# Normalizing q by an accumulating DMA and one exp, in place of transposes

## The chip, the cores and the metric

The kernel runs on one core of a Trainium2 chip. The metric is device time in microseconds of one launch. The core has engines with their own instruction queues: TensorE (PE in the profile, its weight loads PEld), VectorE (DVE), ScalarE (ACT), GpSimd (POOL), and SyncE (SP), which here only issues DMAs.

## The reference

Eight batches of a linear attention are followed by a gated projection. All is float32 on the inputs (batch 8, heads 8, tokens 576, head dimension 64); the three weights arrive as float64.

```python
q_s = q - np.max(q, axis=-1, keepdims=True)
q_s = np.exp(q_s)
q_s = q_s / (np.sum(q_s, axis=-1, keepdims=True) + 1e-09)
k_s = k - np.max(k, axis=2, keepdims=True)
k_s = np.exp(k_s)
k_s = k_s / (np.sum(k_s, axis=2, keepdims=True) + 1e-09)
kv = np.einsum('bhsd,bhse->bhde', k_s, v)
x = np.einsum('bhsd,bhde->bhse', q_s, kv)      # then [batch, token, 512 channels]
...
for k in range(5):                             # causal taps over the tokens
    gate_pre += conv_w[k] * xp[:, k:k + S, :]
gate = 1.0 / (1.0 + np.exp(-gate_pre))
val = x @ w_val
return gate * val @ w_out
```

So q is normalized over the 64 channels of a head, for each token; k over the tokens, for each channel.

## The kernel before

Batches are worked on one after the other, and a batch's later stages overlap the next batch's first ones. The 512 channels are four blocks of 128 (two heads each); the 576 tokens are 512 main ones (four chunks of 128) and a tail of 64, two batches' tails sharing one tile of 128 partitions.

**k and kv.** k's maxima over the tokens come from a channel-major copy of k (steps load_km, k_peak), pass through a DRAM row and come back broadcast to all partitions (k_row, k_spread); k_sub and k_exp then work on token-major k. Batches 0 and 1 instead exponentiate the channel-major copy and transpose it on TensorE (load_kc, k_top, k_raise, k_turn). kv multiplies k by v, whose extra column of ones gives the sum; kv_norm writes kv / sum as a block-diagonal 128 x 128 tile for each channel block (tile kvd).

**q.** q is loaded token-major (load_q); q_max reduces each head, q_sub subtracts, q_exp takes exp, q_sum adds up and takes the reciprocal, q_mul scales. q_turn transposes the chunks on TensorE into PSUM (tile qTps, eight 128 x 128 transposes a group, two groups a batch), q_turned copies them to SBUF as channel-major q; tail_turn and tail_turned do the tails of two batches. Batch 0 subtracts its maximum in PSUM (q_lift, q_minus, q_raise).

**attend.** x = kvd^T q, channels on partitions and tokens along the row. For batch 0 it is one float32 product of 512 columns. For the others q and kv are split into a float32r high part and a low rest (q_turned and q_low; kv_high and kv_low) and three products are added up. The 64 tail columns are one float32 product more.

**Gate and projections.** x_high and x_low split x into float32r parts (tiles xh, xl). first and tap build the causal convolution (five taps; on DVE, or as ACT product and POOL addition), sigmoid follows. value(b, m) multiplies the four channel blocks of x by one block of w_val: 3 products x 4 blocks x 2 halves of 288 tokens = 24 matmuls (line L542). gated multiplies with the gate, g_high and g_low split again (gh, gl), project does the same 24 matmuls with w_out, store copies out of PSUM and issues the store.

**Weights.** They arrive as pairs of 32-bit words; part, field, scaled, signed and joined build float32 from them, w_high and w_low split it. Eight slabs (load_words 0 to 7), four for each matrix, and slab 8 for the taps.

**What sets the order.** ORDER, a list written out by hand, is walked from front to back; each step puts its instructions at the end of its engines' queues. A letter behind a step names its engine: a is ACT, v DVE, p POOL. All DMAs of the kernel before are issued by SP, in that order as well: one that waits for its data holds those behind it. Tile pools add waits: a step that takes a tile whose buffers are all in use waits for the last reader of the oldest. Pools that matter here are words (4 buffers; also kvs and qTlo), xh and xl (6 each), gate (6), g and o (2 each), qT (1), and PSUM's two tags "x" (attend, q_turn) and "mm" (kv, value, project), two banks each. An order step "warm n" issues n transposes that nobody reads.

## Time and profile before

| | |
|---|---|
| median of 3 runs | 321.03 us (320.58 to 323.54) |
| the profiled execution | 320.3 us, its span 318.5 us |
| granted TensorE clock, mean | 0.995 |
| busy share: PE, DVE, ACT, POOL | 93%, 85%, 64%, 59% |
| DMA moved | 51.25 MB, 161 GB/s over the span |

Busy time of an engine is the time in which it executes; a high share tells that the engine has little room, but what it is worth to relieve it depends on the stretch. The chain of waits goes back from the last instruction and puts each piece of the span down to what released it. The windows cut the span in stretches and give each engine's busy time in them, so that stretches with different limits can be told apart. In the timeline a row is one instruction, or several of one kind in a row (x2), with its start, its duration, and, in brackets, how long its engine had idled before it and what released it. Matmuls overlap in the timeline, so that their cost is read from start to start.

### The profile page before, as it was taken

How to read it: one execution, taken by the hardware profiler on the slowest of the kernel's cores; microseconds unless marked ns; L12 is line 12 of the kernel's file. 1: busy time of each engine (PE TensorE's matmuls, PEld its weight loads, DVE VectorE, ACT ScalarE, POOL GpSimd, SP SyncE). 2: the span in 40 equal slices, each digit the busy share in tenths (PEclk: the TensorE clock that was granted, in tenths of full speed). 3: DMA queues.
4: the chain of work that ended last, by engine and by line, in shares of the span. 5: the costliest groups of instructions: out<-in, count | busy, mean ns of one | idle time of the engine just before them, and what ended most of it. 6: DMA issues, size and time to landing. Idle time of an engine off the chain costs nothing.

```text
span 318.5 us, 6426 instructions
## 1 busy us (share of the span) xinstructions
PE 297.3 (93%) x2557; PEld 276.4 (87%) x2557; DVE 271.5 (85%) x374; ACT 204.6 (64%) x316; POOL 188.7 (59%) x157
## 2 busy tenths in 40 slices
PE   2897689989899989999999999999999999999995
...
GB/s 250 370 390 174 410 396 199 194 8 175 238 264 264 74 181 139 254 189 112 143 64 313 50 232 283 160 16 355 82 0 37 39 77 2 0 74 76 0 42 108
DMA packets 20525, 51.25 MB, mean 161 GB/s; under 512 B 2832, under 2 KB 7312, under 8 KB 17808
## 3 DMA queue, kind: packets, MB, share of 16 engines
...
q8 instruction: 20, 0.33, 0.4%
...
HBM read 41.39 MB, written 9.45 MB: 160 GB/s over the span
## 4 chain that ended last, share of the span: by engine, by line
PE 55%; DVE 19%; DMA 16%; issue 4%; ACT 4%; SPq 1%; DVEq 0%; ACTq 0%
PE out L542 22%; PE val L542 20%; DVE gate L524 5%; DMA km<-in_k_strided 5%; PE x L498 4%; PE kv L433 4%; DMA words<-in_w_out 3%; DMA out<-o 2%; DMA q<-in_q 2%; DMA q<-in_q_tail 2%; PE qTps L465 2%; DVE qm L347 2%; DVE g L563 2%; DVE qs L362 2%; DVE kpk L274 2%
## 5 line engine op out<-in xcount | busy, mean ns | idle before, releaser
L524 DVE SCALAR_TENSOR_TENSOR gate<-x,cw,gate 128x575 f32<-128x575 f32 (+3 forms) x99 | 78.0, 807 | 3.3 <-POOL gate L528 1.5
L528 POOL TENSOR_TENSOR gate<-gate,far 128x572 f32<-128x572 f32 (+3 forms) x29 | 39.5, 1363 | 39.2 <-ACT far L527 38.9
L542 PE MATMUL out<-gh,w_out_lo 128*128 128x288 f32 x256 | 57.0, 301 | 0.7 <-ACT gh L160 0.7
L542 PE MATMUL val<-xh,w_val_lo 128*128 128x288 f32 x256 | 56.5, 302 | 0.8 <-DVE o L162 0.7
L542 PE MATMUL out<-gl,w_out_hi 128*128 128x288 f32 x256 | 55.6, 296 | 0.9 <-DVE gl L571 0.9
L542 PE MATMUL val<-xl,w_val_hi 128*128 128x288 f32 x256 | 55.0, 296 | 0.9 <-DVE xl L518 0.9
L542 PE MATMUL out<-gh,w_out_hi 128*128 128x288 f32 x256 | 55.4, 295 | 0.0
L542 PE MATMUL val<-xh,w_val_hi 128*128 128x288 f32 x256 | 54.8, 295 | 0.0
L571 POOL TENSOR_TENSOR gl<-g,gh 128x576 fp32r<-128x576 f32 x25 | 36.8, 1476 | 29.5 <-ACT gh L160 23.1
L542 PEld LDWEIGHTS out<-gl,w_out_hi 128*128 128x128 f32 x256 | 41.4, 188 | 1.4 <-DVE gl L571 1.4
L542 PEld LDWEIGHTS val<-xh,w_val_lo 128*128 128x128 f32 x256 | 40.9, 188 | 1.8 <-DVE o L162 0.9
L542 PEld LDWEIGHTS val<-xl,w_val_hi 128*128 128x128 f32 x256 | 41.2, 188 | 1.2 <-DVE xl L518 1.2
L542 PEld LDWEIGHTS out<-gh,w_out_lo 128*128 128x128 f32 x256 | 41.2, 189 | 1.0 <-ACT gh L160 1.0
L542 PEld LDWEIGHTS out<-gh,w_out_hi 128*128 128x128 f32 x256 | 41.5, 188 | 0.0
L542 PEld LDWEIGHTS val<-xh,w_val_hi 128*128 128x128 f32 x256 | 41.3, 188 | 0.0
L389 POOL TENSOR_TENSOR q<-q,qs 128x512 f32<-128x512 f32 x25 | 26.2, 1070 | 14.7 <-DVE qs L364 14.7
L563 DVE TENSOR_TENSOR g<-val,gate 128x576 f32<-128x576 f32 x32 | 23.9, 749 | 9.9 <-PE val L542 7.3
L527 ACT ACTIVATE far<-x,cw 128x572 f32<-128x572 f32 (+3 forms) x29 | 21.0, 737 | 14.2 <-DVE gate L524 9.3
L160 ACT CAST gh<-g 128x576 fp32r<-128x576 f32 x25 | 16.7, 672 | 17.5 <-DVE g L563 17.4
L160 ACT COPY o<-out 128x576 f32<-128x576 f32 (+1 forms) x22 | 13.5, 618 | 22.1 <-PE out L542 12.1
L531 ACT ACTIVATE gate<-gate 128x576 f32<-128x576 f32 x32 | 21.6, 685 | 6.1 <-DVE gate L524 3.5
L289 POOL TENSOR_TENSOR k<-k,kmax 128x512 f32<-128x512 f32 x18 | 24.9, 1397 | 0.9 <-DMA kmax<-krow 0.9
...
## 6 DMA issues: line engine op xcount, KB each, us to landing
...
q<-in_q SPq DMA_DIRECT2D x7, 1024.0 KB, 7.4
...
k<-in_k SPq DMA_DIRECT2D x6, 1024.0 KB, 7.5
...
words<-in_w_out SPq DMA_DIRECT2D x4, 512.0 KB, 11.8
```

Source lines behind the costliest of these rows:

```text
L160: nc.scalar.copy(out=out, in_=in_)
L289: engine(e).tensor_sub(kk[r, cs], kk[r, cs], mx[r, cs])
L389: engine(e).tensor_mul(qq, qq, s.unsqueeze(2).broadcast_to([P, H, D]))
L433: nc.tensor.matmul(acc[h * D:(h + 1) * D, p, :], T["k", b][:, c, cs] if c < 4 else ktz[b % 2][:, cs], T["v", b][:, c, hd] if c < 4 else T[ ...
L498: nc.tensor.matmul(ps[:, :MAIN], a, z, start=(i == 0), stop=(i == len(parts) - 1))
L524: nc.vector.scalar_tensor_tensor(out=a, in0=x, scalar=w, in1=a, op0=ALU.mult, op1=ALU.add)
L527: nc.scalar.activation(part, x, AF.Copy, scale=w)
L528: nc.gpsimd.tensor_add(a, a, part)
L531: nc.scalar.activation(T["gate", b, p], T["gate", b, p], AF.Sigmoid)
L542: nc.tensor.matmul(ps[:, cs], a[:, kb, ms], z[kb][:, cs], start=(kb == 0 and i == 0), stop=(kb == NB - 1 and i == 2),)
L563: nc.vector.tensor_mul(T["g", b, m], T["val", b, m], T["gate", b, m])
L571: engine(e).tensor_sub(T["gl", b, m], T["g", b, m], T["gh", b, m].bitcast(F32))
```

## The change

**q, batches 2 to 7.** Token-major q is still loaded, and q_max, q_sub, q_exp and q_sum still run, but only for the numbers: q_log takes the logarithm of the sums (ACT) and combines it with the maxima to -(max) - log(sum) (DVE). q_row transposes these numbers (at most 40 columns) on TensorE, copies them to SBUF and writes them to DRAM rows by four small DMAs of SP (and two more for the tails of a pair). q_in loads raw q again, channel-major, 1.18 MB, into the tile qTs (two buffers). q_spread adds the numbers to it by two DMAs issued from POOL's queue, which read each row broadcast to the 64 channels of its head. q_last takes exp of the tile, 2304 elements a partition. Since exp(q - max - log(sum)) is the normalized value, q_mul, q_turn, q_turned, q_low and the tail steps go for these batches.

**attend, all batches.** Two float32 products of 288 columns each (kvd times the whole channel-major q), in place of the three float32r products of 512 and the tail's 64; kv_high and kv_low go.

**Batches 0 and 1.** They keep the transposes of q. Batch 0's path through PSUM goes; q_max, q_exps and q_sum work on pieces of q that are loaded in another order. Each of the two batches has its own tail_turn.

**Buffers and tables.** The f tiles (load_km, weight parts) have four buffers and not three; xh and xl are halves of one "pair" tile, whose six buffers the weight words use as well; g and o have three. Maxima that are needed negated come negated from the reduction. One set of ACT tables that holds exp and logarithm is loaded by name ahead of the first use after a sigmoid.

**The order.** ORDER is written anew throughout. Three places show it. The first is DVE around the last steps of batch 0 ahead of its first value product. Before (gate is tap of batch 0 in its channel block, xl is x_low, e are weight words, ks is kv_norm of batch 1):

```order
L249 TENSOR_SCALAR e_350<-e_350 128x512
L250 SCALAR_TENSOR_TENSOR e_350<-words_348,e_350 128x512
L524 SCALAR_TENSOR_TENSOR gate_0_417<-x_0_399,cw,gate_0_417 128x572
L524 SCALAR_TENSOR_TENSOR gate_2_512<-x_2_462,cw,gate_2_512 128x575
L249 TENSOR_SCALAR e_391<-e_391 128x512
L250 SCALAR_TENSOR_TENSOR e_391<-words_203,e_391 128x512
L518 TENSOR_TENSOR xl_2_535<-x_2_462,xh_2_522 128x576
L443 TENSOR_SCALAR ks_539<-kv_465 128x4
L444 RECIPROCAL ks_539<-ks_539 128x4
L524 SCALAR_TENSOR_TENSOR gate_2_512<-x_2_462,cw,gate_2_512 128x574
L518 TENSOR_TENSOR xl_3_555<-x_3_515,xh_3_531 128x576
```

After (qm is q_max of batch 2, kpk is k_peak of batch 2, x_0_1 <- x_1 is x_low of channel block 1):

```order
L352 TENSOR_REDUCE qm_463<-q_410 128x40
L511 SCALAR_TENSOR_TENSOR gate_1_432<-x_1_402,cw,gate_1_432 128x572
L278 TENSOR_REDUCE kpk_149<-km_2_420 128x1
L511 SCALAR_TENSOR_TENSOR gate_1_432<-x_1_402,cw,gate_1_432 128x573
L505 TENSOR_TENSOR x_0_1_438<-x_1_402,x_0_1_438 128x576
L511 SCALAR_TENSOR_TENSOR gate_1_432<-x_1_402,cw,gate_1_432 128x574
L511 SCALAR_TENSOR_TENSOR gate_1_432<-x_1_402,cw,gate_1_432 128x575
L511 SCALAR_TENSOR_TENSOR gate_0_446<-x_0_423,cw,gate_0_446 128x573
L511 SCALAR_TENSOR_TENSOR gate_0_446<-x_0_423,cw,gate_0_446 128x574
L253 TENSOR_SCALAR e_428<-e_428 128x512
L254 SCALAR_TENSOR_TENSOR e_428<-words_375,e_428 128x512
L511 SCALAR_TENSOR_TENSOR gate_0_446<-x_0_423,cw,gate_0_446 128x575
```

The whole of q_max 2 and a k_peak of batch 2 stand ahead of batch 0's taps and of x_low; x_low of blocks 0, 3 and 2 follow in rows 73, 77 and 78 of DVE's list, where before the last one is row 70.

The second place is TensorE from the end of a projection to batch 2's first attend. Before it is preceded by transposes; these are the rows from batch 1's last value product before its attend (val is value 0 3, x_0 and x_1 are attend):

```order
L542 MATMUL val_3_697<-xh_3_531,w_val_hi 128x288 x2
L542 MATMUL val_3_697<-xl_3_555,w_val_hi 128x288 x2
L498 MATMUL x_0_730<-qT_695,kvs_594 128x512 x2
L498 MATMUL x_0_730<-qTlo_0_728,kvs_594 128x512
L499 MATMUL x_0_730<-qTt_375,kvd_80 128x64
L498 MATMUL x_1_755<-qT_695,kvs_594 128x512 x2
L498 MATMUL x_1_755<-qTlo_0_728,kvs_594 128x512
L499 MATMUL x_1_755<-qTt_375,kvd_80 128x64
L542 MATMUL out_0_790<-gh_0_675,w_out_lo 128x288 x2
```

After, the end of project 0 1 and attend 2 0, with the next value product behind it:

```order
L530 MATMUL out_1_1042<-gl_2_758,w_out_hi 128x288 x2
L530 MATMUL out_1_1042<-gh_3_811,w_out_lo 128x288 x2
L530 MATMUL out_1_1042<-gh_3_811,w_out_hi 128x288 x2
L530 MATMUL out_1_1042<-gl_3_837,w_out_hi 128x288 x2
L486 MATMUL x_0_1072<-qT_699,kvd_78 128x288 x2
L530 MATMUL val_0_1081<-x_1_0_829,w_val_lo 128x288 x2
L530 MATMUL val_0_1081<-x_1_0_829,w_val_hi 128x288 x4
```

An attend has two matmuls, not four, reads kvd and one tile of q, and no transposes of q stand among the batches from 2 on.

The third place is POOL around the first accumulating DMA. Before, the end of batch 0's g_low (gl), with kv_low (kvs) and q_sub of batch 2 (q) between, and the last weight slabs (f, w_out_lo):

```order
L571 TENSOR_TENSOR gl_0_691<-g_0_586,gh_0_675 128x576
L459 TENSOR_TENSOR kvs_594<-kvd_80,kvs_594 128x512
L351 TENSOR_TENSOR q_372<-q_372,qm_689 128x512
L262 TENSOR_TENSOR w_out_lo<-f_518,w_out_hi 128x4x128
L571 TENSOR_TENSOR gl_1_769<-g_1_722,gh_1_739 128x576
L254 TENSOR_TENSOR f_724<-e_590,f_724 128x512
L351 TENSOR_TENSOR q_372<-q_372,qm_689 128x512
L254 TENSOR_TENSOR f_776<-e_747,f_776 128x512
L351 TENSOR_TENSOR q_372<-q_372,qm_689 128x512
L262 TENSOR_TENSOR w_out_lo<-f_776,w_out_hi 128x4x128
```

After (k and kt are k_sub of batch 2, the three q are q_sub of batch 3, DMA is q_spread of batch 2):

```order
L293 TENSOR_TENSOR kt_237<-kt_237,kmax_514 64x512
L559 TENSOR_TENSOR gl_2_758<-g_2_670,gh_2_748 128x576
L559 TENSOR_TENSOR gl_0_820<-g_0_701,gh_0_732 128x576
L356 TENSOR_TENSOR q_664<-q_664,qm_742 128x512 x3
L559 TENSOR_TENSOR gl_3_837<-g_3_755,gh_3_811 128x576
L356 TENSOR_TENSOR q_664<-q_664,qm_742 128x512
L423 DMA qT_699<-qrow_793 64x4x576 x2
L258 TENSOR_TENSOR f_841<-e_809,f_841 128x512
L159 CAST w_out_hi<-f_841 128x4x128
L266 TENSOR_TENSOR w_out_lo<-f_841,w_out_hi 128x4x128
```

The four g_low of batch 0 are no longer all on POOL, those that are stand behind k_sub of batch 2, and the last weight slab's joined, w_high and w_low are issued behind the accumulating DMA.

The core of the diff (of the order one line each):

```diff
-KM = 3
-F32_BATCHES = (0,)
+KM, QT = 4, 2
+FIRST = 2
...
-    g_low 1 2 p, value 1 3, attend 2 1, q_low 2 1, attend 2 0, x_high 2 1 a, gated 1 3, q_max 3, first 2 1 a,
+    signed 7, q_sub 3 2 p, q_spread 2, joined 7 p, w_high 7 p, tap 1 0 0 v, x_low 1 0, project 0 2, x_low 1 1,
...
+    def pair(name, dtype):
+        return work.tile([P, 2 * S], dtype, tag="pair", name=name, bufs=6)
...
+    def exponentials():
+
+        if T["table"] != "exp":
+            nc.scalar.preload_act_table_set("natural_log_exp_and_others")
+            T["table"] = "exp"
...
-            T["words", i] = small.tile([P, n, 2], I32, tag="words", name=f"words{i}", bufs=4)
+            T["words", i] = pair(f"words{i}", I32)[:, :2 * C].rearrange("p (n t) -> p n t", t=2)
...
-        nc.vector.tensor_reduce(out=T["qm", b][:, cs], in_=qq, axis=AX.X, op=ALU.max)
+        nc.vector.tensor_reduce(out=T["qm", b][:, cs], in_=qq, axis=AX.X, op=ALU.max, negate=b < 2)
...
-        nc.vector.reciprocal(s, s)
+        if b < FIRST:
+            nc.vector.reciprocal(s, s)
...
-    def q_lift(b, g):
...
-    def q_minus(b, g):
...
-    def q_raise(b, g):
...
+    def q_log(b):
+        n = q_parts(b) * H
+        s, m = T["qs", b][:, :n], T["qm", b][:, :n]
+        exponentials()
+        nc.scalar.activation(s, s, AF.Ln)
+        t = T["ql", b] = small.tile([P, 5 * H], F32, tag="ql", name=f"ql_{b}")
+        nc.vector.scalar_tensor_tensor(t[:, :n], m, -1.0, s, op0=ALU.mult, op1=ALU.subtract)
+
+    def q_row(b, e="a"):
+        n = q_parts(b) * H
+        ps = bank(f"qlT_{b}", "x")
+        nc.tensor.transpose(ps[:n, :P], T["ql", b][:, :n], ident)
+        o = T["qlT", b] = small.tile([5 * H, P], F32, tag="qlT", name=f"qlT_{b}")
+        copied(e, o[:n], ps[:n, :P])
+        if b % 2 == 0:
+            for x in (b, b + 1):
+                T["qrow", x] = rowpool.tile([H, S], F32, tag=f"qrow{x}", name=f"qrow{x}")
+        for c in range(4):
+            nc.sync.dma_start(out=T["qrow", b][:, c * P:(c + 1) * P], in_=o[c * H:(c + 1) * H])
+        if b % 2 == 0:
+            for x in (b, b + 1):
+                nc.sync.dma_start(out=T["qrow", x][:, MAIN:], in_=o[4 * H:, rows(x)])
+
+    def q_in(b):
+        T["qT", b] = work.tile([P, NB, S], F32, tag="qTs", name=f"qT_{b}", bufs=QT)
+        nc.sync.dma_start(out=T["qT", b], in_=qc[b - FIRST])
+
+    def q_spread(b):
+        for half in range(2):
+            src = T["qrow", b].rearrange("(n x) t -> x n t", x=2)[half].unsqueeze(0).broadcast_to([64, NB, S])
+            nc.gpsimd.dma_start(out=T["qT", b][64 * half:64 * half + 64], in_=src, accum_op=ALU.add, max_dma_last_dim=S * 4)
+
+    def q_last(b, h="a"):
+        exponentials()
+        t = T["qT", b][:, {"a": slice(0, 4), "l": slice(0, 2), "r": slice(2, 4)}[h]]
+        nc.scalar.activation(t, t, AF.Exp)
...
-    def kv_high(b, e="a"):
...
-    def kv_low(b, e="v"):
...
-            T["qT", b] = work.tile([P, NB, MAIN], F32 if b in F32_BATCHES else F32R, tag="qT", name=f"qT_{b}")
-        copied(e, T["qT", b][:, 2 * g:2 * g + 2], T["qps", b, g].rearrange("p (n s) -> p n s", n=2))
-
-    def q_low(b, g):
-        lo = T["qTlo", b, g] = small.tile([P, 2, MAIN], F32R, tag="words", name=f"qTlo_{b}_{g}", bufs=4)
-        hi = T["qT", b][:, 2 * g:2 * g + 2].bitcast(F32)
-        nc.vector.tensor_sub(lo, T["qps", b, g].rearrange("p (n s) -> p n s", n=2), hi)
+            T["qT", b] = work.tile([P, NB, S], F32, tag="qTs", name=f"qT_{b}", bufs=QT)
+        copied(e, T["qT", b][:, 2 * g:2 * g + 2, :MAIN], T["qps", b, g].rearrange("p (n s) -> p n s", n=2))
 
     def tail_turn(b):
-        if b % 2 == 0:
-            ps = T["qtps", b] = bank(f"qTtps_{b}")
-            for p in range(NB):
-                nc.tensor.transpose(ps[:, p * P:(p + 1) * P], T["q", b][:, 4, p * P:(p + 1) * P], ident)
+        ps = T["qtps", b] = bank(f"qTtps_{b}")
+        for p in range(NB):
+            nc.tensor.transpose(ps[:, p * P:(p + 1) * P], T["q", b - b % 2][:, 4, p * P:(p + 1) * P], ident)
 
     def tail_turned(b, e="a"):
-        if b % 2 == 0:
-            T["qTt", b] = T["qTt", b + 1] = work.tile([P, NB, P], F32, tag="qTt", name=f"qTt_{b}", bufs=1)
-            copied(e, T["qTt", b], T["qtps", b][:, :MAIN].rearrange("p (n s) -> p n s", n=NB))
+        if ("qT", b) not in T:
+            T["qT", b] = work.tile([P, NB, S], F32, tag="qTs", name=f"qT_{b}", bufs=QT)
+        i = T["qtps", b][:, :MAIN].rearrange("p (n s) -> p n s", n=NB)[:, :, rows(b)]
+        copied(e, T["qT", b][:, :, MAIN:], i)
 
     def attend(b, p):
-
-        ps = bank(f"x_{b}_{p}", "x")
-        qh = T["qT", b][:, p]
-        if b in F32_BATCHES:
-            parts = ((kvd[b % 2][:, p], qh),)
-        else:
-            hi, lo = (T["kvs", b][:, i, p * P:(p + 1) * P] for i in range(2))
-            parts = ((lo, qh), (hi, qh), (hi, T["qTlo", b, p // 2][:, p % 2]))
-        for i, (a, z) in enumerate(parts):
-            nc.tensor.matmul(ps[:, :MAIN], a, z, start=(i == 0), stop=(i == len(parts) - 1))
-        nc.tensor.matmul(ps[:, MAIN:S], kvd[b % 2][:, p], T["qTt", b][:, p, rows(b)], start=True, stop=True)
-        T["x", b, p] = ps[:, :S]
+        T["x", b, p] = halved_bank(f"x_{b}_{p}", "x")
+        for cs in tokens("a"):
+            nc.tensor.matmul(T["x", b, p][:, cs], kvd[b % 2][:, p], T["qT", b][:, p, cs], start=True, stop=True)
...
-        xh = T["xh", b, p] = block("xh", f"xh_{b}_{p}", 6, F32R)
+        T["xx", b, p] = pair(f"x2_{b}_{p}", F32R)
+        xh = T["xh", b, p] = T["xx", b, p][:, :S]
...
-        xl = T["xl", b, p] = block("xl", f"xl_{b}_{p}", 6, F32R)
+        xl = T["xl", b, p] = T["xx", b, p][:, S:]
...
-        T["g", b, m] = block("g", f"g_{b}_{m}", 2)
+        T["g", b, m] = block("g", f"g_{b}_{m}", 3)
...
-            T["o", b, n] = block("o", f"o_{b}_{n}", 2)
+            T["o", b, n] = block("o", f"o_{b}_{n}", 3)
```

269 lines of the change are left out of this document (117 added, 152 removed).

## The prediction

> **What bounds the kernel now.** I read the page's first part and its slices first, then the chain of waits, then the windows by stage, then TensorE's own waits.
>
> ```profile
> span 318.5 us, 6426 instructions
> PE 297.3 (93%) x2557; PEld 276.4 (87%) x2557; DVE 271.5 (85%) x374; ACT 204.6 (64%) x316; POOL 188.7 (59%) x157
> PE   2897689989899989999999999999999999999995
> ...
> PE 55%; DVE 19%; DMA 16%; issue 4%; ACT 4%; SPq 1%; DVEq 0%; ACTq 0%
> ```
>
> TensorE is busy 93% of the span and nearly without a gap in the second half, but it holds only 55% of the chain that ended last: the rest, DVE and DMA, must lie where TensorE is not full. The windows say where. Columns: window, its length, then busy time and instructions of PE, PEld, DVE, ACT, POOL, the granted clock, the DMA share, GB/s.
>
> ```profile
> 0.00:45.50 45.50, 33.54 (x277) 20.69 (x277) 37.97 (x66) 35.45 (x65) 22.25 (x26) 0.96 0.90 327
> 45.50:80.00 34.50, 32.90 (x238) 31.66 (x237) 32.28 (x43) 24.25 (x45) 30.07 (x24) 1.00 0.54 164
> 80.00:120.00 40.00, 36.72 (x373) 34.59 (x373) 36.17 (x47) 31.25 (x47) 27.03 (x23) 1.00 0.66 205
> 120.00:160.00 40.00, 39.23 (x301) 37.71 (x299) 38.31 (x47) 30.71 (x47) 30.55 (x26) 1.00 0.49 163
> ...
> 200.00:240.00 40.00, 40.00 (x359) 39.10 (x358) 37.33 (x46) 25.60 (x33) 26.37 (x21) 1.00 0.32 112
> ...
> 300.00:318.50 18.50, 15.30 (x115) 15.06 (x114) 3.70 (x6) 2.70 (x5) 1.43 (x1) 1.00 0.18 65
> sum 318.50, PE 297.25 PEld 276.36 DVE 271.52 ACT 204.55 POOL 188.67; mean PE 33.03 PEld 30.71 DVE 30.17 ACT 22.73 POOL 20.96
> ```
>
> So there are two stages. After 45.5 us TensorE works 297.25 − 33.54 = 263.7 of 273.0 us. The last window lacks 3.2 us (the last copy and store), which leaves 6.1 us of waits in 270. Before 45.5 us DVE (38.0 of 45.5) and DMA (0.90 busy, 327 GB/s) are the full ones. The boundary is the first value product:
>
> ```profile
> 44.45 1.12 PE L498 MATMUL x<-qT,kvd 128*128 128x512 f32 x2 [0.69 <-DVE gate L524]
> 45.41 0.33 PE L499 MATMUL x<-qTt,kvd 128*128 128x64 f32 x2
> 45.55 0.52 PE L542 MATMUL val<-xh,w_val_lo 128*128 128x288 f32 x2
> 45.90 0.42 PE L542 MATMUL val<-xh,w_val_hi 128*128 128x288 f32 x2
> ...
> 46.43 0.43 PE L542 MATMUL val<-xh,w_val_lo 128*128 128x288 f32 x2
> ...
> 47.74 0.75 DVE L518 TENSOR_TENSOR xl<-x,xh 128x576 fp32r<-128x576 f32 x1
> ```
>
> The time is therefore: start 45.5 + TensorE's work 263.7 + its waits 6.1 + tail 3.2 = 318.5 us of span, and 1.8 around it in this execution (320.3). The median, 321.03, lies 0.7 above that; I work in the execution's terms and add 0.7 at the end.
>
> **TensorE's work after the start.** Removed are the transposes of q for batches 2 to 7 (two groups of eight a batch) and the tail transposes of the pairs from 2, 4 and 6.
>
> ```profile
> 93.48 0.60 PE L481 MATMUL qTtps<-ident,q 128*128 128x128 f32 x4
> 93.91 1.91 PE L465 MATMUL qTps<-ident,q 128*128 128x128 f32 x16
> 95.91 0.54 PE L542 MATMUL val<-xh,w_val_lo 128*128 128x288 f32 x2
> ```
>
> Start to start, two groups take 95.91 − 93.91 = 2.00 us, a tail 0.43: 12 × 1.00 + 3 × 0.43 = −13.3 us. Attention changes form for the 28 products of batches 1 to 7: three passes of 512 columns and a tail of 64 become two float32 products of 288.
>
> ```profile
> 239.28 0.64 PE L498 MATMUL x<-qT,kvs 128*128 128x512 f32 x2
> 239.75 0.40 PE L498 MATMUL x<-qTlo,kvs 128*128 128x512 f32 x1
> 239.99 0.33 PE L499 MATMUL x<-qTt,kvd 128*128 128x64 f32 x2
> 240.12 0.71 PE L498 MATMUL x<-qT,kvs 128*128 128x512 f32 x2
> 240.67 0.39 PE L498 MATMUL x<-qTlo,kvs 128*128 128x512 f32 x1
> 240.90 0.33 PE L499 MATMUL x<-qTt,kvd 128*128 128x64 f32 x2
> 241.04 0.52 PE L542 MATMUL out<-gh,w_out_lo 128*128 128x288 f32 x2
> ```
>
> The old form takes 0.84 (239.28 to 240.12) and 0.92, mean 0.88. A float32 product of 288 columns is not in the trace; batch 0's float32 form is: 0.96 for 512 columns (44.45 to 45.41), 0.14 for 64. A straight line through both gives 0.55 for 288, so 1.10 for a new attend: 28 × 0.22 = +6.2 us. The bounds are 0.88 (no change) and 2 × 0.96 (no gain from fewer columns; +29 us), which the 64-column product excludes. The six new transposes of the log rows cost a quarter of a tail each, about 0.1: +0.6. Sum: **−6.5 us**, TensorE's work becomes 257.2.
>
> **The start.** TensorE also loses batch 0's lift of q in PSUM there, which frees nothing: DVE and DMA set the start. DVE's list ahead of batch 0's last x_low grows. By durations of the same kinds of row, what DVE executes up to its last x_low adds up to 44.7 us before and 50.3 after. The two causes are work of later batches that now stands ahead of it: five channel maxima of k (batches 2 and 3) and batch 2's maximum of q.
>
> ```profile
> L274 DVE TENSOR_REDUCE kpk<-km 128x1 f32<-128x576 f32 x24 | 17.7, 742 | 4.1 <-DMA km<-in_k_strided 4.1
> L347 DVE TENSOR_REDUCE qm<-q 128x40 f32<-128x2560 f32 x3 | 8.4, 2810 | 0.0
> L475 DVE TENSOR_TENSOR qTlo<-qTps,qT 128x1024 fp32r<-128x1024 f32 x14 | 16.7, 1214 | 0.5 <-ACT qT L160 0.5
> ```
>
> 5 × 0.742 + 2.81 = 6.5 us; the shorter reductions, the eight dropped negations and the moved q_mul nearly cancel. ACT's list grows as well, by scalings of eight instructions each (the other rows here are used further down):
>
> ```profile
> L531 ACT ACT_TABLE_LOAD x8 | 10.3, 1283 | 0.9 <-DVE gate L524 0.7
> ...
> L387 ACT ACTIVATE q<-q,qs 128x64 f32<-128x64 f32 x32 | 8.1, 341 | 2.2 <-DVE qs L364 2.2
> ...
> L355 ACT ACTIVATE q<-q 128x2560 f32<-128x2560 f32 x3 | 7.0, 2345 | 0.0
> ...
> L389 POOL TENSOR_TENSOR q<-q,qs 128x512 f32<-128x512 f32 x25 | 26.2, 1070 | 14.7 <-DVE qs L364 14.7
> ```
>
> Before there are 32 of these; now there are 40, all ahead of the first value product. The lag is bounded by 0 (DVE idles 7.5 us in the first window, which could absorb it) and by 8 (with the same idle, and batch 1's product of k and v placed ahead of the first value product). I take **+5**, near the sum of rows, since most of that idle is the wait for the first load, which stays.
>
> **What comes back.** The 6.5 us that DVE does early are missing from its list between 45.5 and 120 us, where TensorE waits 1.6 + 3.3 us, and 14 q_low of 1.21 us (16.7 us) go altogether. Two waits of TensorE name exactly those:
>
> ```profile
> PE x L498 <- DVE qTlo L475: 1.1, 2, 0.7
> PE x L498 <- ACT far L527: 1.1, 1, 1.1
> PE val L542 <- DVE xl L518: 0.9, 1, 0.9
> PE out L542 <- DVE gl L571: 0.9, 1, 0.9
> ```
>
> I take **−2** of the 6.1: what is late next is the first project, whose last g_low stands on POOL behind batch 2's k_sub and q_sub. ACT's 14 casts of q go against six long exps, six logs, eight scalings and four table loads of 1.28 us more; at 64% share they lie beside TensorE's work, and if ACT were short, each load would cost up to its 1.28. The third buffers of g and o can only remove waits. POOL loses 21 scalings of 1.07 us and gains ten q_sub, ten casts, ten tap additions and twelve DMA issues; an issue there is not in the trace; I bound it by nothing and by one scaling, so 0 to 13 us over 270, hidden while POOL stays near 60%.
>
> **The accumulating DMAs.** New are six loads of 1.18 MB, six small row writes, and twelve DMAs of 590 KB on POOL's queue that read a DRAM row broadcast to 64 partitions and add. None of that kind is in the trace; the nearest rows are:
>
> ```profile
> q<-in_q SPq DMA_DIRECT2D x7, 1024.0 KB, 7.4
> ...
> kmax<-krow SPq DMA_DIRECT2D x6, 256.0 KB, 4.8
> ```
>
> At the q load's rate the pair takes 1.18/1.05 × 7.4 = 8.3 us. At kmax's rate, a broadcast read from DRAM as these are, a half takes 11 and a pair in sequence 22. I take the first, since both halves are long runs like q's. The cover is TensorE's work between the issue and the first attend that reads the result, less the exp (2304 elements of each partition, by q's exp of 2560 in 2.35 us some 2.1). A value or project is 24 products of 0.133 (45.90 to 46.43 holds four), 3.2 us. By the order, four projects and two attends stand between for batch 2 (15.0), four blocks for batch 3 (12.8), four and one attend for batch 5 (13.9), five or more for the others: covers of 12.9, 10.7, 11.8, and 15 or more. A pair of 8.3 us costs **0**.
>
> The Trainium skill, DMA: Bandwidth & Descriptors, section "Anatomy of one DMA — SWDGE (gpsimd) path", fits a DMA from GpSimd by about 2.0 us plus its bytes at 436 GB/s; that gives an estimate of 3.4 us for a half, below my row, and the same sum; no run here shows it for an accumulating one.
>
> **Forecast.** 320.3 − 6.5 + 5 − 2 = 316.8, and 0.7 for the median: **317.5 us**.
>
> **Rivals.**
>
> *The start is not later.* DVE's idle absorbs the additional rows and the first value product stays near 45.5 to 47. For it: 7.5 us of idle. Against it: ACT's and DMA's lists grow there too, with DMA at 0.90. Time: 317.5 − 5 − 1.5 (more waits gone) = 311.
>
> *The accumulating DMAs land late* (the other side). Place: attend of batches 2, 3 and 5, which wait for q_last, which waits for the pair. It decides from 10.7 us a pair. At 15 us the three are late by 2.1, 4.3 and 3.2: +9.6, 327; at 22 us all six batches wait and it is 20 us and more worse. For it: kmax's 4.8 us for 256 KB, and DMA shares of 0.5 to 0.66 until 200 us. Against it: after 200 us the share is 0.32 and less. A reason for late landing of its own is that POOL's issue is held while DVE works: DVE is 90% busy up to 160 us. The Trainium skill, SBUF — State Buffer, section "SBUF: two separate sides", has this as a trap: DVE operations that use both its SBUF ports keep GpSimd from writing descriptors, so that a DMA from its queue seems blocked; before has no such DMA, so the trace neither agrees nor disagrees.
>
> *The start lags by 8 and the first project waits as before.* 320.3 − 6.5 + 8 − 1 + 0.7 = 321.5: no change. For it: POOL's 30.1 of 34.5 us between 45.5 and 80, the place where g_low of batch 0 now stands behind six subtractions.
>
> **How the numbers follow.** Forecast 0.47, within 314.5 and 320.5; start not later 0.24; late DMAs 0.21; lag of 8 with no gain 0.08. About 1% is what a measurement can tell from no change: 317.8 and 324.2 are the bounds. The forecast's cases split at 317.8, 0.24 below and 0.23 above. Faster: 0.24 + 0.24 = 0.48. Slower: late DMAs from 14 us a pair, 0.19. Same: 0.23 + 0.08 + 0.02 = 0.33. The range, 310 to 327, takes in the first rival whole and the second up to 15 us; left out are its worse half and the far edges. The likeliest case's own range is 314.5 to 320.5.
>
> **What would show it.** TensorE's instructions after the first value product should sum to about 257 us; the two products of 288 columns should take 1.10 start to start; the first value product should start between 49 and 53 us; no wait of TensorE should name an attend on ACT's q_last. Wrong would be: the first value product before 47.5 us (first rival), a wait of more than 1 us at the attends of batches 2, 3 and 5 with DMA behind it (second), or POOL's g_low ahead of the first project by 3 us (third).

## The result

| | before | after |
|---|---|---|
| median | 321.65 us (320.58 to 323.54) | 334.38 us (331.08 to 334.83) |
| the profiled execution | 320.3 us, span 318.5 us | 334.44 us, span 332.7 us |

The ratio of the times is 1.041, with a 95% interval of 1.036 to 1.046: the changed kernel is 4% slower, where 317.5 us and a range up to 327 were forecast. The page of the changed kernel, with its lines on busy time, the slices of TensorE and of its clock, and the chain of waits:

```profile
span 332.7 us, 6157 instructions
PE 282.5 (85%) x2390; PEld 265.2 (80%) x2390; DVE 253.7 (76%) x350; ACT 210.7 (63%) x319; POOL 192.2 (58%) x168
PE   0046277996997999699899999999999999999994
PEclk9999965999997999899999999999999999999998
PE 66%; DMA 13%; DVE 8%; ACT 4%; SPq 3%; issue 2%; POOL 1%; DVEq 0%; POOLq 0%; ACTq 0%
```

TensorE works 14.8 us less than before and DVE 17.8 us less, and the span is 14.2 us longer. The losses stand in the first half: TensorE does nothing in the first two slices (17 us) and little in the fifth (33 to 42 us), and three gaps follow, in the slices from 75, 100 and 133 us; in the last two the granted clock drops to 7 and 8 tenths as well, and from 42 to 58 us it is 6 and 5. The windows, split at the first value product of each kernel (columns as in the prediction), put numbers to it. Of the changed kernel:

```profile
0.00:60.20 60.20, 25.49 (x240) 20.40 (x240) 50.83 (x81) 45.08 (x100) 42.65 (x45) 0.89 0.80 290
60.20:332.70 272.50, 256.99 (x2154) 244.85 (x2150) 202.82 (x270) 165.62 (x220) 149.57 (x124) 0.98 0.57 176
```

and of before, whose first row the prediction has shown:

```profile
45.50:318.50 273.00, 263.72 (x2283) 255.67 (x2281) 233.55 (x309) 169.10 (x252) 166.42 (x131) 1.00 0.40 133
```

So the first value product comes 14.7 us later; TensorE's instructions behind it are busy for 6.7 us less; and what is left of the second stage, waits and tail, is 15.5 us in place of 9.3, 6.2 more. The sum, 14.7 − 6.7 + 6.2, is the 14.2 us by which the span grew. Of the 6.2 us, 4.9 are waits of TensorE (11.0 for 6.1), and 1.3 are the tail from the end of its last matmul (4.5 us, 328.2 to 332.7, for 3.2, 315.3 to 318.5). TensorE's own waits, of the whole span (columns: engine and line, what it waited for, us in total, how often, the longest):

```profile
PE x L486 <- ACT kvd L459: 7.2, 1, 7.2
PE x L486 <- ACT qT L428: 5.5, 2, 2.9
PE x L486 <- DVE gate L511: 3.5, 1, 3.5
PE out L530 <- DVE gl L559: 2.3, 2, 1.4
```

The first and the third lie in the start, ahead of the first value product. The second, of 5.5 us, are two attends that wait for q_last: those of batches 2 and 3. The timeline of POOL, ACT and TensorE around these two (rows of batch 2, then of batch 3, and the page's row on these DMAs with its median from issue to landing):

```profile
82.86 1.21 POOL L423 DMA_DIRECT2D qT<-qrow  x1
100.03 2.12 ACT L428 ACTIVATE qT<-qT 128x2304 f32<-128x2304 f32 x1 [3.75 <-issue]
102.20 2.29 PE L486 MATMUL x<-qT,kvd 128*128 128x288 f32 x4 [2.86 <-ACT qT L428]
122.46 1.01 POOL L423 DMA_DIRECT2D qT<-qrow  x1
136.81 2.12 ACT L428 ACTIVATE qT<-qT 128x2304 f32<-128x2304 f32 x1 [3.12 <-DMA out<-o]
138.98 1.41 PE L486 MATMUL x<-qT,kvd 128*128 128x288 f32 x3 [2.67 <-ACT qT L428]
qT<-qrow POOLq DMA_DIRECT2D x12, 576.0 KB, 9.1
```

From the issue of a pair to the start of its exp pass 17.2 and 14.3 us, where the prediction had 8.3 for the pair. The exp stands behind other things on ACT, so I also took the packets of the pair from the trace: batch 2's move from 86.8 to 99.4 us, 12.7 us, while the core's other queues move 2.4 MB; batch 4's take 7.2 us beside 0.1 MB. A wait costs more than its length, as the windows show that hold the attends behind the two waits of the start and the two on q_last:

```profile
40.00:45.00 5.00, 2.74 (x6) 2.01 (x7) 4.93 (x9) 3.50 (x11) 3.76 (x3) 0.54 0.54 182
50.00:55.00 5.00, 3.26 (x10) 2.61 (x11) 4.89 (x9) 4.71 (x14) 3.35 (x3) 0.57 0.30 120
100.00:105.00 5.00, 2.79 (x7) 2.22 (x8) 4.90 (x10) 4.94 (x5) 5.00 (x5) 0.69 0.96 399
140.00:145.00 5.00, 5.00 (x24) 4.12 (x24) 4.06 (x3) 3.37 (x6) 1.49 (x2) 0.72 0.66 227
```

Behind each of the four idle stretches of 7.2, 3.5, 2.86 and 2.67 us the granted clock (the number ahead of the DMA share) is far below 1.00: TensorE starts again at half speed. In the kernel before no wait behind the start is longer than 1.1 us, and its clock stays at 1.00.

The longer tail comes from the order of the last copies. The last product is copied out of PSUM in two halves; before copies one of them at 310.58 us, while TensorE still works, and one copy is left for the tail (first row, of before). The changed kernel copies both behind the last matmul, the second waiting for the first (the other rows):

```profile
315.34 0.40 ACT L160 COPY o<-out 128x288 f32<-128x288 f32 x1 [4.35 <-PE out L542]
...
328.24 0.46 DVE L159 COPY o<-out 128x288 f32<-128x288 f32 x1 [5.62 <-PE out L530]
328.77 0.40 ACT L157 COPY o<-out 128x288 f32<-128x288 f32 x1 [1.45 <-DVE o L159]
```

### The profile page after: what moved, and what is told of

It is laid out like the page before. It is cut to its first block, busy times and chain, and to the rows that moved or that the text cites. A ratio compares the mean times of both kernels' runs of the same rounds, so it can differ in the third digit from the quotient of the medians.

```text
span 332.7 us, 6157 instructions
## 1 busy us (share of the span) xinstructions
PE 282.5 (85%) x2390; PEld 265.2 (80%) x2390; DVE 253.7 (76%) x350; ACT 210.7 (63%) x319; POOL 192.2 (58%) x168
## 4 chain that ended last, share of the span: by engine, by line
PE 66%; DMA 13%; DVE 8%; ACT 4%; SPq 3%; issue 2%; POOL 1%; DVEq 0%; POOLq 0%; ACTq 0%
PE val L530 28%; PE out L530 24%; PE x L486 9%; DMA kc<-in_k_channels 5%; PE kv L441 4%; DMA qT<-qrow 3%; DMA out<-o 2%; DMA q<-in_q_tail 2%; DVE e L254 1%; ACT qT L428 1%; DVE gl L559 1%; DMA qrow<-qlT 1%; DVE gate L511 1%; DVE e L253 1%; ACT far L514 1%
## 5 line engine op out<-in xcount | busy, mean ns | idle before, releaser
L515 POOL TENSOR_TENSOR gate<-gate,far 128x575 f32<-128x575 f32 (+3 forms) x39 | 52.1, 1337 | 79.1 <-ACT far L514 78.6
L530 PE MATMUL val<-x,w_val_hi 128*128 128x288 f32 x512 | 89.2, 296 | 0.0
L511 DVE SCALAR_TENSOR_TENSOR gate<-x,cw,gate 128x572 f32<-128x572 f32 (+3 forms) x89 | 71.4, 809 | 6.1 <-POOL gate L515 2.6
L530 PEld LDWEIGHTS val<-x,w_val_hi 128*128 128x128 f32 x512 | 75.8, 189 | 0.0
L530 PE MATMUL val<-x,w_val_lo 128*128 128x288 f32 x256 | 58.1, 308 | 0.4 <-DVE g L551 0.4
L486 PE MATMUL x<-qT,kvd 128*128 128x288 f32 x128 | 42.5, 472 | 16.8 <-ACT kvd L459 7.2
L486 PEld LDWEIGHTS x<-qT,kvd 128*128 128x128 f32 x128 | 26.0, 217 | 24.6 <-ACT kvd L459 7.3
L530 PEld LDWEIGHTS val<-x,w_val_lo 128*128 128x128 f32 x256 | 42.3, 191 | 2.1 <-PE val L530 0.6
L514 ACT ACTIVATE far<-x,cw 128x575 f32<-128x575 f32 (+3 forms) x39 | 28.5, 740 | 20.7 <-DVE gate L511 16.2
L559 POOL TENSOR_TENSOR gl<-g,gh 128x576 fp32r<-128x576 f32 x19 | 29.2, 1539 | 12.7 <-ACT gh L157 11.4
L356 POOL TENSOR_TENSOR q<-q,qm 128x512 f32<-128x512 f32 x23 | 28.3, 1307 | 5.1 <-DVE qm L352 3.4
L499 ACT ACTIVATE gate<-x,cw 128x576 f32<-128x576 f32 x25 | 18.4, 741 | 13.3 <-PE x L486 11.8
L157 ACT CAST x<-x 128x576 fp32r<-128x576 f32 x28 | 17.8, 638 | 12.1 <-DVE gate L501 5.5
```

Source lines behind the costliest of these rows:

```text
L157: nc.scalar.copy(out=out, in_=in_)
L356: engine(e).tensor_sub(qq, qq, T["qm", b][:, cs].unsqueeze(2).broadcast_to([P, H, D]))
L486: nc.tensor.matmul(T["x", b, p][:, cs], kvd[b % 2][:, p], T["qT", b][:, p, cs], start=True, stop=True)
L499: nc.scalar.activation(a, x, AF.Copy, scale=w)
L511: nc.vector.scalar_tensor_tensor(out=a, in0=x, scalar=w, in1=a, op0=ALU.mult, op1=ALU.add)
L514: nc.scalar.activation(part, x, AF.Copy, scale=w)
```

## Experiments

The kernels differ from the changed kernel in nothing but what the diffs show, unless they are said to be built on before. Ratios are to the kernel before, measured beside each of them, with the 95% interval; the changed kernel's is 1.041 (1.036 to 1.046).

### The accumulating DMAs

**The additions left out.** No accumulating DMA is issued, so q isn't normalized; all else, the rows of numbers too, stays.

```diff
-        for half in range(2):
+        for half in range(0):
```

> The changed kernel without the twelve accumulating DMAs (q_last takes exp of raw q, so x is not normalized): everything else stays. If they are what makes batches 2 and 3 late (attends wait 2.9 and 2.7 us for q_last, and TensorE runs at half clock for 3.4 us behind each), the waits and the half clock go: 5.6 + 3.4 = 9 us, about 325 to 326, and the first value product stays at 60. If the waits are due to ACT's queue or to the q loads, less than 2 us are gained.

It takes 325.71 us, ratio 1.016 (1.009 to 1.023). Its window behind the first value product, at 60.67 us:

```profile
60.67:323.40 262.73, 253.51 (x2154) 242.65 (x2150) 200.00 (x270) 165.31 (x220) 138.69 (x113) 1.00 0.44 156
```

No wait on q_last is left, TensorE works 3.5 us less at a clock of 1.00, and waits and tail are 262.73 − 253.51 = 9.2 us (4.8 and 4.4), where before has 9.3 (6.1 and 3.2). So the twelve DMAs cost 9.3 us of span (332.7 − 323.4): 6.3 of waits and 3.5 of slow clock, less 0.5 in the start. The late start and the smaller work of TensorE are untouched by them.

**Issued earlier.** q_spread 2 goes ahead of q_sub of batch 3 on POOL; q_in, q_row and q_spread of batch 3 go some 30 steps ahead.

```diff
-... g_low 0 3 p, k_spread 3, ..., q_sub 3 2 p, q_spread 2, joined 7 p ...
+... tap 1 1 1 v, q_spread 2, q_sub 3 3 p, q_sub 3 0 p, ...
-... first 2 1 a, tap 2 1 0 v, q_in 3, ..., q_row 3 a, ..., first 2 2 a, q_spread 3 ...
+... tap 1 2 3 v, q_in 3, q_row 3 a, ..., value 1 1, q_spread 3 ...
```

> The changed kernel with batch 2's accumulating DMAs issued ahead of POOL's four subtractions of batch 3 (3 us earlier), and batch 3's row transpose, its load of raw q and its accumulating DMAs some two value products earlier (12 us). Nothing else moves. Theory lateness (the attends of batches 2 and 3 wait because the pair is issued too late for the 14 to 17 us that it takes beside other loads): the waits of 2.9 and 2.7 us and the half clock behind them go, 6 to 9 us, 326 to 328. Rival contention (an earlier pair only meets more of the other loads and lands no sooner): less than 2 us.

It takes 335.48 us, ratio 1.046 (1.039 to 1.052): no gain, and none behind the first value product either (272.7 us for 272.4). Batch 3's attend waits only 0.5 us, but POOL now holds its queue for the rows of numbers, and project 0 waits for a g_low that is queued behind it:

```profile
POOL qT L419 <- DMA qrow<-qlT: 4.3, 1, 4.3
PE out L526 <- POOL gl L555: 4.1, 1, 4.1
```

This wait of TensorE ends at 88.85 us, and half clock comes with it too (87 to 94 us). Only batch 3's part was worth keeping, and it is in the combinations below.

### DVE held by POOL in the start

DVE's steps up to the last x_low of batch 0 keep it busy for 40.9 us before (to 48.5 us) and 50.6 after (to 60.0). Of the growth, 3.7 us are the weight words (14.8 us for 11.1), although there are 22 such steps and not 23. The timeline of DVE, with POOL's rows of the same time behind it:

```profile
36.98 1.42 DVE L254 SCALAR_TENSOR_TENSOR e<-words,e 128x512 int32<-128x512 int32 x1
38.77 1.63 DVE L254 SCALAR_TENSOR_TENSOR e<-words,e 128x512 int32<-128x512 int32 x1
41.98 1.48 DVE L253 TENSOR_SCALAR e<-e 128x512 int32<-128x512 int32 x1
...
36.81 1.04 POOL L388 TENSOR_TENSOR q<-q,qs 128x512 f32<-128x512 f32 x1 [0.46 <-DVE qs L371]
38.54 1.31 POOL L258 TENSOR_TENSOR f<-e,f 128x512 int32<-128x512 int32 x1 [0.69 <-DVE e L254]
41.86 1.32 POOL L258 TENSOR_TENSOR f<-e,f 128x512 int32<-128x512 int32 x1
```

The same two kinds of row in before:

```profile
17.36 0.43 DVE L249 TENSOR_SCALAR e<-e 128x512 int32<-128x512 int32 x1
17.82 0.69 DVE L250 SCALAR_TENSOR_TENSOR e<-words,e 128x512 int32<-128x512 int32 x1
```

An instruction of 0.69 us takes 1.42 or 1.63, one of 0.43 takes 1.48, and each ends 0.3 to 0.6 us behind the POOL instruction beside it (37.85, 39.85 and 43.18 us). The Trainium skill, SBUF — State Buffer, section "SBUF: two separate sides", tells of a pair of ports that DVE and GpSimd hold in turn, each for a whole instruction. The rows agree: DVE's three end no later than one undisturbed duration behind POOL's.

**Five scalings from POOL to ACT.**

```diff
-scaled 8 p, ... part 8 p, ... scaled 4 p, ... part 0 p, ... part 4 p
+scaled 8 a, ... part 8 a, ... scaled 4 a, ... part 0 a, ... part 4 a
```

> The changed kernel with the five scalings of weight words that POOL does in the start (scaled 8 and 4, part 8, 0 and 4) on ACT, as most of them were before. Theory POOL holds DVE (in the trace DVE's integer steps of 0.42 and 0.69 us take 1.0 to 1.6 between 25 and 43 us, each ending with a POOL instruction): about half of the POOL work of 25 to 42 us goes, DVE is 2 to 4 us shorter ahead of its last x_low and the time falls by as much, about 331. Theory list (it is the number of steps, not their length): 334 to 335, as ACT gets 3 us more in the start.

332.31 us, ratio 1.035 (1.028 to 1.042). The interval overlaps that of the changed kernel, so the time alone decides nothing. The first value product comes 1.7 us earlier, at 58.52, but that is little more than it moves without any change to the start: 60.20 us in the changed kernel, 60.67 and 61.61 in the two runs above, whose edits lie behind it. DVE's rows decide: its weight words take 11.2 us for 14.8, about what they took before, and the window shows DVE with 47.84 us for 50.83 and POOL with 35.15 for 42.65:

```profile
0.00:58.50 58.50, 26.20 (x240) 21.37 (x240) 47.84 (x81) 46.43 (x105) 35.15 (x39) 0.88 0.86 299
```

**The reverse, in the kernel before:** the same five scalings from ACT to POOL.

```diff
-scaled 8 a, ... part 0 a, ... part 8 a, ... part 4 a, ... scaled 4 a
+scaled 8 p, ... part 0 p, ... part 8 p, ... part 4 p, ... scaled 4 p
```

> The kernel before with the same five scalings of weight words on POOL that the changed kernel has there (in its order, letters alone changed). Theory POOL holds DVE: DVE's word steps ahead of the first value product grow from 10.7 us by 2 to 4, the first value product comes at 47 to 49, time 322 to 324. If POOL's instructions do not lengthen DVE's: at most 1 us through the later weights, 321.

325.66 us, ratio 1.013 (1.006 to 1.020): here the loss shows in the time, some 4 us, and the first value product comes at 49.05 us for 45.55. Five instructions on an engine that is half idle there (22.25 of 45.5 us) cost 4 us. DVE's rows divide the 3.5 us of the start:

```profile
43.19 1.26 DVE L245 TENSOR_SCALAR e<-e 128x512 int32<-128x512 int32 x1 [0.71 <-POOL e L164]
44.48 1.63 DVE L246 SCALAR_TENSOR_TENSOR e<-words,e 128x512 int32<-128x512 int32 x1
```

DVE waits 0.7 us because the words come later from POOL, and its two steps take 1.8 us longer than in before (0.42 and 0.69); the x_low behind them is 2.5 us late (48.62 us for 46.09). The remaining 1.0 us falls where TensorE, behind a wait of 3.3 us for DVE, has a clock of 0.69 (45 to 50 us).

### The other links of the start

**TensorE kept busy.** 40 transposes that nobody reads behind kv 0, 20 ahead of attend 0 3.

```diff
-tail_turned 0 a, k_top 1 2, kv 0, k_top 1 3,
+tail_turned 0 a, k_top 1 2, kv 0, warm 40, k_top 1 3,
-tap 0 0 2 v, attend 0 3,
+tap 0 0 2 v, warm 20, attend 0 3,
```

> The changed kernel with 40 idle transposes on TensorE behind batch 0's kv and 20 ahead of attend 0 3, where its trace shows TensorE idle for 7.2 and 3.5 us and then at half clock (0.54 to 0.77 between 40 and 60 us). Theory clock (the half clock makes the chain attend, k_turn, attend, kv ahead of the first value product 3.5 us longer): first value product near 57 instead of 60.2, time 3 to 4 us lower, about 331. Theory list (DVE's list sets the start, x_low of block 2 ends at 60.0 whatever the clock): first value product at most 1 us earlier and its later products wait for x_low, time within 1.5 us of 334.4.

It takes 338.24 us, ratio 1.057 (1.049 to 1.064). The time at half clock in the start halves (13.7 to 6.8 us by the clock's records), but these transposes need PSUM banks themselves, and two new waits follow:

```profile
PE x L483 <- ACT o L154: 4.4, 1, 4.4
PE warm L576 <- ACT ktz L154: 3.0, 1, 3.0
```

What a full clock in the start would be worth is therefore not measured.

**Shorter maxima.** q_max of batch 2 looks at 8 of 64 channels, and k_peak of batches 2 and 3 at 64 of 576 tokens; the subtracted values aren't the maxima then.

```diff
-in_=qq, ...            in_=T["km", b, j]
+in_=qq[:, :, :8] if b == 2 else qq, ...   in_=T["km", b, j][:, :64] if b < 4 else T["km", b, j]
```

> The changed kernel in which batch 2's maximum of q is taken over 8 of the 64 channels and batches 2's and 3's maxima of k over 64 of the 576 tokens (any number in place of the maximum cancels in a softmax; this leaves out most of the work of these steps, and moves nothing). Of what DVE does ahead of batch 0's last x_low, 2.81 + 5 x 0.74 = 6.5 us become about 1.2. Theory list (the reordered start is late because DVE does later batches' work in it): first value product 4 to 5 us earlier, at 55 to 56, and the time lower by as much, 329 to 330. Rival (TensorE's own chain at half clock, or DMA, sets the start): first value product at 59 or later, time 333 to 335.

332.84 us, ratio 1.030 (1.023 to 1.038). DVE loses 5.5 us of work ahead of the first value product, and that comes only 0.7 us earlier, at 59.48: most of the freed time becomes idle time, and the first attend, at 41.87 us for 42.26, waits as long as it did.

```profile
0.00:59.50 59.50, 24.71 (x241) 20.10 (x241) 45.30 (x81) 45.51 (x101) 42.32 (x45) 0.89 0.84 294
41.87 1.81 PE L482 MATMUL x<-qT,kvd 128*128 128x288 f32 x3 [7.04 <-ACT kvd L455]
```

This is the term that the prediction had as the main cause of the later start (6.5 us of maxima): by itself it is worth no more than the first value product moves between runs of one start.

**The loads in another order.** v of batch 0 and the k that batch 1 lacks are loaded earlier, the k of batches 2 and 3, with their maxima, later.

```diff
-load_km 2 3, ... load_km 3 1, ... k_peak 2 3, ... load_km 2 0, ... load_kt 2, ... load_v 0 m, load_v 0 t, ... k_peak 2 0, load_kc 1 2, ... k_peak 3 1,
+load_kc 1 1, load_kc 1 2, load_v 0 m, load_v 0 t, ... load_words 5, load_km 2 3, load_km 3 1, load_km 2 0, load_kt 2, ... k_peak 2 3, k_peak 2 0, k_peak 3 1,
```

> The changed kernel with v of batch 0 and the third kc of batch 1 loaded right behind the other kc, and the three km and kt of batches 2 and 3 behind the weight slabs, their k_peaks with them. Theory loads: batch 0's kv starts 2 to 4 us earlier, DVE no longer waits for kc, attend 0 1 at 38 to 39 instead of 42, first value product 3 to 4 us earlier, time 330 to 331. Rival ACT (kv 0 waits for copies that stand behind 8 us of scalings on ACT): kv 0 stays at 32, less than 1 us.

336.16 us, ratio 1.045 (1.033 to 1.056). The first attend comes 4.2 us earlier, and the third one gives it all back, since DVE now has its taps behind the moved maxima:

```profile
38.06 1.24 PE L482 MATMUL x<-qT,kvd 128*128 128x288 f32 x4 [2.00 <-ACT kvd L455]
PE x L482 <- DVE gate L507: 11.0, 1, 11.0
```

**Both.** With the short maxima added, that wait is still 7.4 us in two pieces; 332.85 us, ratio 1.037 (1.032 to 1.042), first value product at 60.66.

> The loads of e11 and the short maxima of e8 together (batch 2's maximum of q over 8 of 64 channels, batches 2's and 3's of k over 64 of 576 tokens). Theory two chains (loads to kv 0 to the first attend, and DVE's list to the taps, each hide the other): first attend at 38, first value product at 54 to 56, time 328 to 330, more than the 1.5 us of e8 and the nothing of e11 together. Rival (a third engine, ACT or POOL, is as long): first value product at 59 or later, 332 to 336.

**Scalings of q from ACT to DVE.** The five q_mul of eight instructions each that ACT had in batches 0 and 1:

```diff
-q_mul 0 1 a, ... q_mul 0 3 a, ... q_mul 0 2 a, ... q_mul 0 4 a, ... q_mul 1 3 a
+q_mul 0 1 v, ... q_mul 0 3 v, ... q_mul 0 2 v, ... q_mul 0 4 v, ... q_mul 1 3 v
```

> The changed kernel with its five ACT scalings of batch 0's and 1's q (8 instructions and 2.0 us each) as one DVE instruction of 0.68 us each. Theory ACT: the copies of k and q that batch 0's kv waits for come up to 6 us earlier, batch 0's kv at 27 to 29 instead of 32.5, attend 0 1 at 38 to 39, time 330 to 331. Rival DVE: DVE's list grows by 3.4 us and the first value product comes by as much later, 336 to 338. Rival loads: v of batch 0 lands near 30, kv 0 gains 2 us at most, 334.

340.24 us, ratio 1.061 (1.052 to 1.069), first value product at 65.53: ACT's list isn't what kv 0 waits for (33.11 us, for 32.53), and what DVE gets more to do ahead of the first value product (56.6 us for 50.8) comes back as 5.3 us:

```profile
0.00:65.50 65.50, 26.86 (x240) 21.57 (x240) 56.59 (x86) 37.19 (x62) 45.64 (x46) 0.84 0.77 267
```

**The start of before spliced in.** The order of before, with its path of q through PSUM, up to the first value product, and behind it what the changed order has left to do.

```diff
-... the changed order up to value 0 2 ...
+... the order of before up to value 0 0, the new attend in place of the old ...
```

> The start of the kernel before (its order up to the first value product, with batch 0's lift of q in PSUM and its warm transposes), and behind it the changed kernel's order without the steps already done; the method is the changed one from batch 2 on, attend in halves throughout. If the reordered start is what costs 14.7 us: first value product at 45 to 47, time 334.4 - 13 = 321 to 322 with the waits at attends 2 and 3 still there. If the early maxima and loads of batch 2 in the changed start are needed by its later steps, they come late instead and the time stays above 328.

339.85 us, ratio 1.061 (1.053 to 1.070). The first value product comes at 51.16 us, 9 earlier, and the kernel is slower: TensorE's waits behind it double, from 11.0 to 22.0 us. What the changed order does ahead for later batches is missing there, as I read it; the two longest waits are:

```profile
PE qTps L498 <- DVE gate L544: 10.0, 1, 10.0
PE val L563 <- DVE g L584: 4.1, 1, 4.1
```

**Less ahead of the first value product.** The accumulating DMAs issued earlier, the five scalings on ACT, q_max 2 and its subtractions behind the last x_low of batch 0, and k_turn 1 0 and kv 1 behind the first value product.

```diff
-joined 3 p, q_max 2, q_sub 2 2 p, ... k_turn 1 0, ... q_sub 2 4 p, ... q_sub 2 3 p, ... k_turned 1 0 a, ... q_sub 2 1 p, ... kv 1,
+x_low 0 2, q_max 2, q_sub 2 2 p, q_sub 2 4 p, q_sub 2 3 p, q_sub 2 1 p, ... value 0 2, ... k_turn 1 0, k_turned 1 0 a, kv 1,
```

> The kernel e5_early with three edits in the start: the five POOL scalings of weight words on ACT, q_max 2 and its four subtractions behind batch 0's last x_low, and batch 1's last k transposes and its kv behind the first value product. Theory list (DVE's and TensorE's lists ahead of the first value product are too long): 2.8 us of DVE, 2 us of DVE stretching and 4 to 6 us of TensorE go from ahead of it, first value product at 54 to 56 instead of 60.2, time 5 to 6 us under e5_early, about 321. Rival (what is moved comes late instead: q_max 2 feeds the chain of batch 2's accumulating DMA): the first value product is earlier, but attend 2 0 waits by as much, no gain over e5_early.

338.34 us, ratio 1.054 (1.049 to 1.060). The first value product comes at 55.52 us, 4.7 earlier, but kv 1 at 63 and the first project at 82 for 77.9: again nothing is left of it.

**Combinations.** The scalings on ACT with batch 3's DMAs earlier:

> The changed kernel with the POOL scalings of weight words on ACT and batch 3's row transpose, load and accumulating DMAs earlier; batch 2's stay where they were (in e5 their earlier place made POOL wait 4.3 us for the row in DRAM, and TensorE's first projection 4.1 us for g_low behind it). Theory: the two gains add, 2 us from the words and 4.4 us from batch 3 (its wait of 2.7 and half of the 3.4 us at half clock): 327 to 329. If batch 3's gain of e5 was only shifted (e5 as a whole gained nothing), 332 as with the words alone.

331.64 us, ratio 1.032 (1.0285 to 1.0360). But for the run without the additions it is the only one whose interval lies below that of the changed kernel (from 1.0362). With the short maxima as well:

> All three at once: short maxima as in e8, the POOL scalings of weight words on ACT, batch 3's accumulating DMAs earlier. If the three causes are separate, their gains add: 5 + 2 + 1, about 326, still above the kernel before. If they are one cause seen three times (DVE's list in the start), no better than e8.

332.60 us, ratio 1.035 (1.029 to 1.040): nothing is added. The loads, the scalings of q on DVE, the words on ACT and batch 3 together:

> Loads and scalings as in e11 and e12, words on ACT and batch 3's DMAs earlier as in e7. If loads and ACT hold the start together (each alone hidden by the other), the sum is more than the parts: first value product at 50 to 53, time 322 to 325. If DVE's list is the bound once both are gone: first value product at 56 to 57, time 328 to 330.

337.02 us, ratio 1.050 (1.044 to 1.056). And the loads, the short maxima, the words and batch 3:

> As e14, with the POOL scalings of weight words on ACT and batch 3's accumulating DMAs earlier. Theory two chains: 2 us from the words and 1 to 4 us from batch 3 on top of e14, 323 to 327. Rival third engine: ACT gets 3 us more in the start, no better than e14.

331.12 us, ratio 1.033 (1.026 to 1.039), first value product at 59.03. Four changes at four links take 1.2 us off the 14.7, no more than the first value product moves between runs of one start.

### The method and the order apart

**The new method in the old order.** Batches 2 to 7 go by the accumulating DMA and one exp, but the steps stand as in before, the steps of q some 10 us earlier.

```diff
-... value 0 3, gated 0 1, q_max 2, ... q_mul 2 0 p, ... q_turn 2 0, ... q_low 2 1, attend 2 0 ...
+... gated 0 2, q_max 2, ... q_in 2, ... q_sum 2, q_log 2, ... q_row 2 a, ... q_spread 2, ... q_last 2 a, ... attend 2 0 ...
```

> The changed method in the order of the kernel before: the start of before with batch 0's lift, all steps of k, gate and projections where they stood, the transposes and splits of q dropped from batch 2 on, attend in halves throughout, and each later batch's q_max, q_sub, q_exp, q_sum some 10 us earlier with log, row, load and accumulating DMAs put between them and its attends. Theory order (the new order's start costs 14 us, the method itself saves TensorE 10): first value product at 46, time 310 to 316. Rival method (the accumulating DMAs come late for any order): first value product at 46, but TensorE waits at the attends of several batches and runs at half clock behind, 320 or more.

395.48 us, ratio 1.234 (1.229 to 1.239). The first value product is at 45.36 us, as before: the method doesn't make the start late, the new order of the start does. Behind it TensorE waits for other engines everywhere, 66.8 us in all, and runs at half clock for 58 us. Three of the longest entries:

```profile
PE x L519 <- ACT far L547: 12.9, 3, 6.8
PE out L563 <- ACT o L153: 9.5, 3, 5.4
PE out L563 <- POOL gl L592: 8.5, 6, 3.9
```

An order that wasn't made for the method says little on what the method is worth; but it can't simply be put into the old one.

**The new attend in the old method.** Before, with its transposes and its order, and attend as two float32 products of 288 columns; q_low, kv_high and kv_low go, and the tiles of the changed kernel come with it.

```diff
-        for i, (a, z) in enumerate(parts):
-            nc.tensor.matmul(ps[:, :MAIN], a, z, start=(i == 0), stop=(i == len(parts) - 1))
-        nc.tensor.matmul(ps[:, MAIN:S], kvd[b % 2][:, p], T["qTt", b][:, p, rows(b)], start=True, stop=True)
+        for cs in tokens("a"):
+            nc.tensor.matmul(T["x", b, p][:, cs], kvd[b % 2][:, p], T["qT", b][:, p, cs], start=True, stop=True)
```

> The kernel before with the change's attention alone: two float32 products of 288 columns per attend for all batches, reading one channel-major tile of q (two buffers); q is still scaled, transposed and copied as before, but q_low, kv_high and kv_low go (16.7 us of DVE, some 3 more of kvs; 2.4 of ACT, 6.8 of POOL); xh and xl share the pair tiles and g and o have three buffers, as in the change. The order is that of before without these steps. By the rows of the changed kernel an attend takes 0.75 to 0.86 start to start against 0.84 to 0.92 before, so TensorE's work falls by 1 to 3 us, and its waits for qTlo (1.1 us) go. If the halves are free, 316 to 319. If they cost the 1.10 that the prediction took, TensorE's work grows by 6 us: 325 to 327.

322.96 us, ratio 1.002 (0.998 to 1.006): the same. By TensorE's rows the two forms of attend cost alike (25.0 and 24.9 us, below), so DVE's 16.7 us of q_low, which the new one saves, show in nothing either.

## Why the prediction was wrong, point by point

**TensorE's work, −6.5: the mechanism held, the attend term was mis-sized.** By the sums of TensorE's rows behind the first value product, each up to the start of the next and with the waits left out, before against the kernel without the additions (so that the clock is 1.00 in both): transposes 13.1 to 1.7, −11.4 for the predicted −13.3; the 28 attends 25.0 to 24.9, −0.1 for the predicted +6.2; rows of logarithms +0.7 for +0.6; the products of the projections, which the prediction left as they were, +0.7. The attend is seen here in the changed kernel:

```profile
72.28 1.13 PE L486 MATMUL x<-qT,kvd 128*128 128x288 f32 x4
73.03 0.51 PE L530 MATMUL val<-x,w_val_lo 128*128 128x288 f32 x1
...
118.63 2.10 PE L486 MATMUL x<-qT,kvd 128*128 128x288 f32 x8
120.35 0.51 PE L530 MATMUL out<-gh,w_out_lo 128*128 128x288 f32 x1
```

0.75 for one, 1.72 for two, and 0.89 on average over the 28: what the old form took (0.89 on average), not 1.10. The straight line through 512 and 64 columns was no price for 288. The transposes were taken at 1.00 a group from one pair; all fourteen groups of before average 0.84. Together −10.2 of work at full clock (263.7 to 253.5). That the trace shows 256.99 us and the prediction 257.2 is chance: 3.5 us of half clock, which it didn't have, fill the place of 3.7 us of work that it had too much.

**The start, +5: the step that failed.** It is +14.7, outside the bounds of 0 and 8. The step added up what DVE executes by durations from undisturbed rows (44.7 to 50.3 us) and left DVE's idle time as it was. Three things were wrong in it. DVE's busy time grew by 9.7 us (40.9 to 50.6) and not 5.6; 3.7 of it are weight words that take longer beside POOL, whose list ahead of the first value product doubles (22.25 to 42.65 us in the first windows). The timeline shows that, and the runs with moved scalings put 1.7 and 3.5 us of start on five such instructions. Second, DVE wasn't the only bound: with 5.5 us less on DVE the start gains 0.7, with the first attend 4.2 us earlier it gains nothing. Third, before starts its first value product 2.2 us ahead of its last x_low; after it stands behind all four, and behind attend 0 3, k_turn 1 0, attend 0 2 and kv 1, which TensorE does from 51.74 us on, in sequence and below full clock (half clock from 50.7 to 57.5 us in the clock's records).

TensorE's rows show besides where the lateness begins. The first row is the start of batch 0's kv in before, the others are TensorE's first row and that kv in the changed kernel:

```profile
22.27 0.69 PE L433 MATMUL kv<-v,k 128*64 128x65 f32 x16
...
20.33 0.42 PE L336 MATMUL ktps<-ident,kc 128*64 128x128 f32 x1 [20.33 <-ACT kc L317]
...
32.53 0.69 PE L441 MATMUL kv<-v,k 128*64 128x65 f32 x16 [1.37 <-ACT qT L157]
```

kv 0 starts 10.3 us later; the first attend, at 42.26 us for 30.00, adds 2.0, and the first value product 2.4. In the changed order batch 0's q_turn and the two tail_turn stand ahead of kv 0 in TensorE's list, in before they stand behind it. In every run with the changed start kv 0 begins between 32.2 and 33.5 us, so no run shows what an earlier kv 0 would be worth. The runs show several chains of nearly the same length (loads to kv 0 and the first attend; DVE's list; POOL's; TensorE's own) that cover each other. So the price of a longer DVE list is what failed, and the new order of the start is shown to cost the 14.7 us (with the old one the same method is at 45.36); how the 10 us or so that POOL's hold on DVE doesn't explain divide among the chains stays open.

**What comes back, −2: 1.3 came, and the tail took it.** Without the additions TensorE's waits are 4.8 us for 6.1; but the tail, which the prediction kept at its 3.2 us without a reason, is 4.4, by the order of the last copies. The relief of DVE by q_low, on which the step relied, is off the path: the run with the new attend in the old method saves q_low and doesn't move.

**The accumulating DMAs, 0: the other step that failed, by the rival named for it.** That rival put a pair of 15 us at +9.6; measured are 17.2 and 14.3 us for batches 2 and 3, and 9.3 us in all. It named batches 2, 3 and 5; batch 5, whose DMAs move beside less traffic (0.7 MB; 11.4 us from the issue on), didn't wait, and in its place came the half clock behind each wait. The q load's rate, from which I took 8.3 us, comes near to a pair alone: in batches 4, 6 and 7, beside 0.1 MB and less, the packets take 6.2 to 8.3 us, and 9.2 to 10.0 pass from the first issue to the last packet. By the fit of the Trainium skill, DMA: Bandwidth & Descriptors, section "Anatomy of one DMA — SWDGE (gpsimd) path", cited in the prediction, two halves in sequence take an estimate of 2 × 3.4 = 6.8 us, less than these pairs from issue to last packet. Beside the 1.8 to 2.4 MB of other loads of batches 3 and 2 the packets take 12.0 and 12.7 us, 13.8 and 16.6 from the issue on. The prediction had the DMA shares of those windows in view, and gave them to the rival instead of to the price.

**The sum.** 318.5 + 14.7 (start) − 10.2 (TensorE's work) − 1.3 (other waits) + 1.2 (tail) + 9.8 (the DMAs behind the start, 6.3 of waits and 3.5 of slow clock) = 332.7 us of span, as measured. The first rival (start not later) and the third (a late g_low on POOL) didn't occur: TensorE's waits for g_low in the changed kernel sum to 2.3 us.

No version that was run beats the kernel before. Whether the method would in an order made for it, with a start as short as that of before, stays open: where the start of before was spliced in, its gain came back as waits.
